# A 640-point spectral transform done as five residue tables instead of four quarter tables and a rest, on one Trainium2 core

## The chip, the cores and the metric

The kernel runs on one core of a Trainium2 chip. A core has five engines with their own instruction queues: TensorE (PE in the profile: matmuls into PSUM; its weight loads are listed apart as PEld), VectorE (DVE), ScalarE (ACT), GpSimd (POOL) and SyncE (SP), which here issues all transfers. Each engine works through its own queue strictly in the order in which the program was written, and an instruction whose input is not ready holds up everything behind it on that engine. The metric is device time in microseconds (us) from the start to the end of one launch. The kernel before takes 212.32 us (median of three runs, 211.74 to 212.51).

## The reference, cut to what matters

Inputs are bf16; x is 1 x 2048 x 640, the spectral weights are 2048 x 321, the feed-forward size is 1536.

```python
xn = layernorm(x)                                            # over the last axis, no gain
X  = rfft2(xn, axes=(-2, -1)) * (w_r + 1j * w_i)             # 2048 x 321, complex
s  = irfft2(X, s=(2048, 640)).astype(bf16)
g  = silu((gelu(xn @ w_gate) * (xn @ w_up)) @ w_down)        # 2048 x 640
return x + s * g
```

Two chains start from the normalised rows: a two-dimensional spectral filter and a gated feed-forward network (FFN). They meet in one product and one sum per element at the end.

## The kernel before

The 2048 rows are split into 16 slabs of 128 rows (row = 16 * n2 + n1; a slab holds one n1). The spectral chain per slab and per group is:

- `fold_a`, `fold_b` (L427, L435; VectorE, two slabs at a time): sums and differences of a row with its mirror images, which turn a 640-point transform along the columns into four real transforms of length 128 and a rest of 128 columns (`fold4`, L419).
- `slab_S1` (L470): five 128x128 matmuls, the transform along n2. ScalarE copies the result out of PSUM.
- `slab_D` (L489, matmuls in `d_matmuls` L479): the transform along the columns. For each of four output quarters one matmul with a 128x161 table `FT` and one with a table `TR` that adds the rest, so eight matmuls of 161 columns a slab. ScalarE copies the result (`zd`, L493), SyncE sends it to a scratch tensor `ZDR`.
- `quad_S2` (L507) and `quad_S2i` (L525), 16 times ("quads"): the 16-point transform over n1, the product with the weights (two VectorE products `p1`, `p2` a quad, L520), and the inverse 16-point transform. ScalarE copies both PSUM results (`xs` L516, `us` L536), and four transfers send `us` to the scratch tensor `UDR`.
- `vfold` (L553), `slab_S1i` (L568), `slab_Di` (L580): the way back, again with a fold, five 128x128 matmuls and eight 161-column matmuls a slab; then two VectorE operations spread the even and odd parts into the output tile `Y` (L587, L588).
- `finish` and `multiply_add` (L601, L594): when a slab of `Y` and of the gate G are both there, two VectorE operations (times G, plus x) and the output transfer follow at once.

The FFN is done in four groups of four slabs: 12 pairs of gate and up matmuls (`ffn_piece` L616: five matmuls of 512 columns each, Gelu on ScalarE into `ge` L628, the product `uT` on VectorE L630), then 4 x 3 `down_third` (L650: eight matmuls of 320 columns), with tanh on ScalarE and one product on VectorE for the gate (`gate_out`, L672; in the last group Silu on ScalarE, and there `multiply_add` comes directly after it).

The order of everything is written out by hand. The list `back` holds 144 steps of FFN work ("slots", numbered from 0); after each slot the items that `put(slot, ...)` has entered for it are emitted, in the order of the calls. So each queue is the slots in order with the spectral work dropped in between. Slots 0 to 35 are FFN group 0, 36 to 71 group 1, 72 to 107 group 2, 108 to 143 group 3. Before the change the forward spectral stage fills slots 3 to 58, the quads 66 to 91, the way back 100 to 134.

Buffers that matter: the PSUM pool `psB` has two buffers, used in turn by every PSUM result of the spectral chain; the FFN has two PSUM buffers for gate (`psg`) and two for up (`psu`), so the third `psu` in a row waits until VectorE has read the first.

```python
for s, b in enumerate(back):                 # L822
    b[0](*b[1:])
    if not any(it[0] is quad_S2 for it in plan[s]):
        flush()
    for it in plan[s]:
        it[0](*it[1:])
    flush()
```

Of the kernel before, what the change touches and what calls it, by code (L numbers as in the profile page):

```python
# [9 lines left out]
FP32 = mybir.dt.float32  # L10
# [65 lines left out]
def build(nc, env):  # L76
    consts, big, wts, xg, work, psA, psB = (env[k] for k in ("consts", "big", "wts", "xg", "work", "psA", "psB"))
# [53 lines left out]
    FT = consts.tile([P, 5, LH], BF16)  # L131
    TR = consts.tile([P, 2, 2, LH], BF16)
# [36 lines left out]
    lint = gtile([LH], INT32)  # L169
    nc.gpsimd.iota(lint, pattern=[[1, LH]], base=0, channel_multiplier=0)  # L170
    vt = gtile([NS, P], INT32)

# [21 lines left out]
    u_f, hi_f, s_f, h_f, g_f, pf, lo_b = bits("pb", [(0, 63), (6, 1), (0, 31), (5, 1), (5, 3), (0, 127), (0, 1)])  # L194
    ph_t = affine("ph_t", hi_f, -1536.0, 1536.0)
    e96 = c1("e96")
    nc.vector.tensor_single_scalar(out=e96, in_=pf, scalar=96.0, op=ALU.is_equal)
    a_m = affine("a_m", pf, 2.0, 64.0)
    b_o = affine("b_o", pf, 1.0, 32.0)
    sp_f = c1("sp_f")  # L200
    nc.vector.tensor_scalar(out=sp_f, in0=e96, scalar1=160.0, scalar2=s_f, op0=ALU.mult, op1=ALU.add)
    b_e = affine("b_e", h_f, -160.0, 160.0)
    a_r = affine("a_r", sp_f, 2.0, 0.0)
    b_r = c1("b_r")
    nc.vector.tensor_scalar(out=b_r, in0=sp_f, scalar1=hi_f, scalar2=b_e, op0=ALU.mult, op1=ALU.add)
# [39 lines left out]
    fv = gtile([3, LH], FP32)  # L245
    ftm = gtile([3, LH], FP32)

    def ft_angle():
        nc.scalar.activation(out=fv[:, 0], in_=lint, func=ACT.Identity, scale=a_m)
        nc.scalar.activation(out=fv[:, 1], in_=lint, func=ACT.Identity, scale=a_m, bias=b_o)  # L250
        nc.scalar.activation(out=fv[:, 2], in_=lint, func=ACT.Identity, scale=a_r, bias=b_r)
        nc.scalar.activation(out=ftm, in_=fv, func=ACT.Identity, scale=1.0 / 640.0, bias=magic)
        nc.scalar.activation(out=ftm, in_=ftm, func=ACT.Identity, bias=nmagic)

    def ft_wrap():
        nc.vector.scalar_tensor_tensor(out=fv, in0=ftm, scalar=-640.0, in1=fv, op0=ALU.mult, op1=ALU.add)

    def ft_sin():
        w = TWO_PI / 640.0 * (1.0 - 2e-7)
        nc.scalar.activation(out=ftm[:, 0:2], in_=fv[:, 0:2], func=ACT.Abs)  # L260
        nc.scalar.activation(out=FT[:, 1:4:2], in_=fv[:, 0:2], func=ACT.Sin, scale=w)
        nc.scalar.activation(out=FT[:, 4], in_=fv[:, 2], func=ACT.Sin, scale=w)
        nc.scalar.activation(out=FT[:, 0:4:2], in_=ftm[:, 0:2], func=ACT.Sin, scale=-w, bias=halfpi)

    def ft_rest():
        nc.gpsimd.memset(mhalf, -0.5)
        mk4 = consts.tile([P, 4], FP32)
        for g in range(4):
            nc.vector.tensor_single_scalar(out=mk4[:, g:g + 1], in_=g_f, scalar=float(g), op=ALU.is_equal)
        for g in range(4):  # L270
            nc.vector.tensor_scalar(out=TR[:, g // 2, g % 2, :], in0=FT[:, 4, :], scalar1=mk4[:, g:g + 1],
                                    scalar2=None, op0=ALU.mult)
        nc.gpsimd.memset(TR[32:33, 0, 0, 0:LH:2], 1.0)
        nc.gpsimd.memset(TR[32:33, 0, 0, 1:LH:2], -1.0)
# [144 lines left out]
    def fold4(dst, src, plus, minus):  # L419
        s4 = src.rearrange("p k (t d) -> p k t d", t=2)  # L420
        dm = dst[:, :, 0:512].rearrange("p k (g d) -> p k g d", g=4)
        dr = dst[:, :, 512:640].rearrange("p k (g d) -> p k g d", g=4)
        for gs, op in ((plus, ALU.add), (minus, ALU.subtract)):
            nc.vector.tensor_tensor(out=dm[:, :, gs, :], in0=s4[:, :, :, 32:160], in1=s4[:, :, :, 288:160:-1], op=op)
            nc.vector.tensor_tensor(out=dr[:, :, gs, 1:32], in0=s4[:, :, :, 1:32], in1=s4[:, :, :, 319:288:-1], op=op)

    def fold_a(pair):  # L427
        xn = X[:, 2 * pair:2 * pair + 2, :]
        assert ("n", 2 * pair + 1) in done
        uvt = work.tile([P, 2, D], BF16, tag="uv", bufs=1)  # L430
        nc.vector.tensor_tensor(out=uvt[:, :, 0:320], in0=xn[:, :, 0:320], in1=xn[:, :, 320:640], op=ALU.add)
        nc.vector.tensor_tensor(out=uvt[:, :, 320:640], in0=xn[:, :, 0:320], in1=xn[:, :, 320:640], op=ALU.subtract)
        xf[pair] = uvt

    def fold_b(pair):  # L435
        uvt = xf[pair]
        f = work.tile([P, 2, D], BF16, tag="xf", bufs=2)
        fold4(f, uvt, slice(0, 4, 3), slice(1, 3))
        nc.vector.tensor_copy(out=f[:, :, 512:D:32], in_=uvt[:, :, 0:D:160])
        xf[pair] = f  # L440
        done.add(("f", pair))

    def chunk(f, k, c):
        return f[:, k, c * P:(c + 1) * P]
# [25 lines left out]
    def slab_S1(n1):  # L470
# [3 lines left out]
        for c in range(5):  # L474
            nc.tensor.matmul(pz[:, c, :], lhsT=chunk(f, n1 % 2, c), rhs=Tfwd[:, n1, :], start=True, stop=True)  # L475
# [3 lines left out]
    def d_matmuls(ps, lhs):  # L479
        for b in range(2):  # L480
            for k in range(2):
                o = ps[:, b, k * LH:(k + 1) * LH]
                nc.tensor.matmul(o, lhsT=lhs[:, 2 * b + k, :], rhs=FT[:, 2 * b + k, :], start=True, stop=False)  # L483
                nc.tensor.matmul(o, lhsT=lhs[:, 4, :], rhs=TR[:, b, k, :], start=False, stop=True)  # L484

    def natural(ps):
        return ps[:, :, 0:LP].rearrange("p b (c m) -> p c m b", c=2)

    def slab_D(n1):  # L489
        pd = psB.tile([P, 2, 512], FP32, tag="b")  # L490
        d_matmuls(pd, Zt.pop(n1))
        zd = work.tile([P, 2, LP], BF16, tag="m2", bufs=3)
        nc.scalar.copy(out=zd.rearrange("p c (m b) -> p c m b", b=2), in_=natural(pd))  # L493
        nc.sync.dma_start(out=ZDR[:, n1].rearrange("c p l -> p c l"), in_=zd[:, :, 0:L])
# [12 lines left out]
    def quad_S2(j):  # L507
# [8 lines left out]
        nc.scalar.copy(out=xs, in_=px[:, :, 0:L])  # L516
        p1 = work.tile([P, 2, L], BF16, tag="p1", bufs=3)
# [7 lines left out]
    def quad_S2i(j):  # L525
# [9 lines left out]
        us = work.tile([P, 2, L], BF16, tag="m2", bufs=3)  # L535
        nc.scalar.copy(out=us, in_=pu[:, :, 0:L])  # L536
        for lo in range(2):
            to = uv[lo][:, j // 8, :, j % 8, :]
            nc.sync.dma_start(out=to[:, :, 0:L], in_=us[lo * 64:lo * 64 + 32, :, :])
            nc.sync.dma_start(out=to[:, :, L:D], in_=us[lo * 64 + 32:lo * 64 + 64, :, 1:320])  # L540
# [12 lines left out]
    def vfold(pair):  # L553
        V = st_c["V"][:, 2 * pair:2 * pair + 2, :]
        f = work.tile([P, 2, D], BF16, tag="xf", bufs=2)
        fold4(f, V, slice(0, 4, 3), slice(2, 0, -1))
# [162 lines left out]
    for n1 in range(4, NS):  # L719
        if n1 == 7:  # L720
            s += 2
# [138 lines left out]
```

## Time and profile before

| | us |
|---|---|
| median of three runs | 212.32 |
| the profiled execution's own time | 212.3 |
| span of the profiled execution (first to last instruction) | 210.5 |
| TensorE busy | 200.3 (95%) |
| VectorE busy | 138.2 (66%) |
| ScalarE busy | 127.7 (61%) |
| GpSimd busy | 19.2 (9%) |

The page of the profile gives busy time by engine, then the span in 40 slices (a digit is the busy share in tenths), the transfer queues, the chain of work that ended last, and the costliest groups of instructions. A group line reads: line of the kernel, engine, operation, output<-input, shape, count, then busy time, the mean duration of one in ns, and the idle time of the engine before it with what ended it. Matmuls and VectorE operations overlap their neighbours at the ends, so the distance from one start to the next is shorter than the duration when nothing is waited for. A timeline line reads: start, duration, engine, line, operation, and in brackets the idle time before it.

### The profile page before, as it was taken

The numbers are of one execution on the slowest core, as the hardware profiler recorded it, in microseconds if no ns is written. First come the engines' busy times: TensorE is split into PE (matmuls) and PEld (weight loads), VectorE is DVE, ScalarE is ACT, GpSimd is POOL, SyncE is SP. The second block draws the span as 40 slices with busy tenths as digits, with TensorE's granted clock in tenths as the row PEclk, the third lists the DMA queues.
The fourth block names the chain that finished last, engine by engine and source line by source line (L and its number), as shares of the span: only waits on it lengthen the run. The fifth ranks groups of instructions, "written<-read, shape, count | busy, mean of one in ns | idle before, by whom it ended". The sixth has DMA issues, their size and how long they took to land.

```text
span 210.5 us, 4486 instructions
## 1 busy us (share of the span) xinstructions
PE 200.3 (95%) x1600; PEld 125.5 (60%) x1600; DVE 138.2 (66%) x436; ACT 127.7 (61%) x215; POOL 19.2 (9%) x53
## 2 busy tenths in 40 slices
PE   0699999999999999999999999999999999999993
PEld 0389984567765555666644434347776556666773
DVE  8878977975975662252566755423769888994443
ACT  7656567599575666532677767732466665665721
POOL 8000128720004000000000000000000000000000
PEclk9999999999999999999999999999999999999999
DMA  5999955765946575739963232328913443332221
GB/s 159 337 361 366 361 159 137 159 165 147 175 78 164 134 175 124 195 120 205 221 131 82 64 86 67 88 68 247 340 42 96 121 120 101 97 93 65 63 78 47
DMA packets 37222, 31.79 MB, mean 151 GB/s; under 512 B 11344, under 2 KB 35024, under 8 KB 37072
## 3 DMA queue, kind: packets, MB, share of 16 engines
q1 hardware_dynamic: 37200, 31.51, 55.5%
q8 instruction: 12, 0.20, 0.4%
q14 instruction: 10, 0.08, 0.1%
HBM read 20.34 MB, written 7.87 MB: 134 GB/s over the span
## 4 chain that ended last, share of the span: by engine, by line
PE 95%; DVE 3%; ACT 1%; issue 0%; POOL 0%; POOLq 0%
PE psg L623 25%; PE psu L623 25%; PE psg L647 13%; PE psu L647 12%; PE pu L533 2%; PE pz L475 2%; PE py L484 2%; PE pd L484 2%; PE pd L483 2%; PE py L483 2%; PE pv L572 2%; PE px L513 2%; PE pw L279 1%; DVE st L371 1%; ACT Tinv L219 1%; PE pt L453 1%
## 5 line engine op out<-in xcount | busy, mean ns | idle before, releaser
L623 PE MATMUL psg<-xnT,Wg 128*128 128x512 bf16 (+1 forms) x275 | 61.5, 355 | 0.0
L623 PE MATMUL psu<-xnT,Wu 128*128 128x512 bf16 (+1 forms) x275 | 61.2, 354 | 0.0
L630 DVE TENSOR_TENSOR uT<-psu,ge 128x512 bf16<-128x512 f32 (+1 forms) x55 | 34.0, 618 | 26.3 <-PE psu L623 25.0
L647 PEld LDWEIGHTS <-uT 128*128 128x128 bf16 x396 | 37.2, 98 | 14.3 <-issue 0.5
L628 ACT ACTIVATE ge<-psg 128x512 bf16<-128x512 f32 (+1 forms) x55 | 30.0, 546 | 20.4 <-PE psg L623 18.9
L623 PEld LDWEIGHTS <-Wg 128*128 128x128 bf16 x275 | 25.6, 99 | 20.0 <-issue 2.3
L623 PEld LDWEIGHTS <-Wu 128*128 128x128 bf16 x275 | 25.6, 99 | 19.7 <-issue 1.8
L647 PE MATMUL psg<-Wd,uT 128*128 128x320 bf16 (+1 forms) x204 | 31.1, 295 | 0.0
L647 PE MATMUL psu<-Wd,uT 128*128 128x320 bf16 (+1 forms) x192 | 28.9, 295 | 0.0
L520 DVE TENSOR_TENSOR p<-xs,W 128x642 bf16<-128x642 bf16 x32 | 14.5, 493 | 9.7 <-ACT xs L516 9.4
L584 ACT ACTIVATE eo<-py 128x644 bf16<-128x644 f32 x16 | 11.3, 707 | 9.8 <-PE py L484 9.6
L516 ACT CAST xs<-px 128x642 bf16<-128x642 f32 x16 | 11.1, 694 | 9.2 <-PE px L513 5.8
L493 ACT CAST zd<-pd 128x644 bf16<-128x644 f32 x16 | 11.1, 694 | 6.0 <-PE pd L484 6.0
L371 DVE BATCH_NORM_STATS2 st<-X 128x6 f32<-128x320 bf16 x32 | 13.9, 477 | 0.0
L596 DVE TENSOR_TENSOR Yall<-Yall,G 128x640 bf16<-128x640 bf16 (+2 forms) x21 | 8.7, 412 | 7.7 <-ACT G L683 7.3
L477 ACT CAST Z<-pz 128x640 bf16<-128x640 f32 x16 | 11.0, 688 | 4.0 <-PE pz L475 4.0
L574 ACT CAST vs<-pv 128x640 bf16<-128x640 f32 x16 | 11.0, 688 | 2.0 <-PE pv L572 2.0
L536 ACT CAST us<-pu 128x642 bf16<-128x642 f32 x16 | 11.2, 700 | 0.9 <-PE pu L533 0.9
L678 DVE SCALAR_TENSOR_TENSOR G<-th,psg 128x320 bf16<-128x320 f32 x12 | 5.8, 482 | 8.8 <-ACT th L677 8.7
L677 ACT ACTIVATE th<-psu 128x320 f32<-128x320 f32 x12 | 5.3, 439 | 8.6 <-PE psu L647 8.5
L483 PE MATMUL py<-FT,vs 128*128 128x161 bf16 x64 | 10.5, 233 | 0.0
L483 PE MATMUL pd<-FT,Z 128*128 128x161 bf16 x64 | 10.5, 233 | 0.0
(140 smaller groups left out, 235.8 us busy)
## 6 DMA issues: line engine op xcount, KB each, us to landing
ZDR<-zd SPq DMA_DIRECT2D x16, 160.5 KB, 3.0
B<-ZDR SPq DMA_DIRECT2D x8, 321.0 KB, 7.2
xt<-in_A_x_dram SPq DMA_DIRECT2D x16, 160.0 KB, 2.4
Wg<-in_B_w_gate_dram SPq DMA_DIRECT2D x4, 480.0 KB, 7.4
Wu<-in_B_w_up_dram SPq DMA_DIRECT2D x4, 480.0 KB, 8.4
X<-in_A_x_dram SPq DMA_DIRECT2D x3, 640.0 KB, 9.1
Wd<-in_B_w_down_dram SPq DMA_DIRECT2D x1, 1920.0 KB, 13.9
Vin<-UDR SPq DMA_DIRECT2D x3, 640.0 KB, 7.6
```

The costliest lines, as they stand in the source:

```text
L371: nc.vector.bn_stats(out=st[:, k, :], in_=xr[:, k, :])
L477: nc.scalar.copy(out=Zt[n1], in_=pz)
L483: nc.tensor.matmul(o, lhsT=lhs[:, 2 * b + k, :], rhs=FT[:, 2 * b + k, :], start=True, stop=False)
L493: nc.scalar.copy(out=zd.rearrange("p c (m b) -> p c m b", b=2), in_=natural(pd))
L516: nc.scalar.copy(out=xs, in_=px[:, :, 0:L])
L520: nc.vector.tensor_tensor(out=pp, in0=xs, in1=WT[j // 8][:, :, j % 8, :], op=ALU.mult)
L536: nc.scalar.copy(out=us, in_=pu[:, :, 0:L])
L584: nc.scalar.activation(out=eo.rearrange("p c (m b) -> p c m b", b=2), in_=natural(py), func=ACT.Copy, scale=(2.0 if n1 >= 12 else 1.0) / ( ...
L623: nc.tensor.matmul(ps, lhsT=WT[:, c, t * P:(t + 1) * P], rhs=xnT[g][:, c, c0:c1_], start=(c == 0), stop=(c == 4))
L628: late.append(lambda: nc.scalar.activation(out=ge, in_=ps, func=ACT.Gelu_apprx_tanh))
L630: nc.vector.tensor_tensor(out=uT[g][:, t, c0:c1_], in0=ps, in1=cur["ge"], op=ALU.mult)
L647: nc.tensor.matmul(ph, lhsT=uT[g][:, t, j * P:(j + 1) * P], rhs=Wd[:, t, c0:c1_], start=(t == 0), stop=(t == NT - 1))
```

## The change

The transform along the columns is taken at half-sample points and split by residues modulo 5. A row of 640 becomes, by sums and differences with its mirror image, an even and an odd half of 320; each half is five blocks of 64. Sums and differences of the blocks and two combinations with the golden ratio (`TAU`, `NU`) leave five full chunks of 128 columns, and each chunk needs one matmul with one full 128x128 table. So `slab_D` and `slab_Di` have five matmuls of 128 columns instead of eight of 161. What goes with it:

- the forward fold has three steps, `fold_a`, `fold_b`, `fold_c`: 2 TENSOR_TENSORs of 640 elements; 2 TENSOR_TENSORs of 512 and 2 SCALAR_TENSOR_TENSORs of 512 (times a constant, plus a tensor, all bf16 in SBUF); 1 TENSOR_TENSOR of 512 and 2 of 256, each needing the one before;
- on the way back there is no `vfold` (the chunks come out of `UDR` as they are needed); after the tables, `spread_a` has 2 SCALAR_TENSOR_TENSORs and 2 TENSOR_TENSORs of 512, `spread_b` has 2 TENSOR_TENSORs of 512 and 2 of 640, a pair of slabs at a time, through a tile `E` with two buffers;
- `quad_S2i` brings `us` into the order of the residues while copying it out of PSUM: two ScalarE copies of 256 elements and a VectorE copy of 256 instead of one ScalarE copy of 642. The products `p1`, `p2` move behind it into a new item `quad_P`. The tiles for `zd` and `us` are three fixed buffers `ZB`;
- a new item `fi_turn` builds the inverse tables from the forward ones by five transposes on TensorE and three ScalarE copies. The rest table `TR` and its VectorE set-up go;
- `multiply_add` of slabs 0 to 11 is no longer done as soon as possible but at slots 106, 112, 118, 124, 130, 132 to 136, 138 and 139. The x tiles for it are kept in the space of `W1`, eight at a time;
- the slots move: folds and tables in new places (forward stage slots 3 to 56, quads 64 to 89, way back 97 to 131), the second Sin table of the forward stage (`tinv_sin`) from slot 22 to 21.

```diff
-    FT = consts.tile([P, 5, LH], BF16)
-    TR = consts.tile([P, 2, 2, LH], BF16)
+    FT = consts.tile([P, 10, 64], BF16)
+    FI = consts.tile([P, 5, P], BF16)
...
     def fold_b(pair):
-        uvt = xf[pair]
-        f = work.tile([P, 2, D], BF16, tag="xf", bufs=2)
-        fold4(f, uvt, slice(0, 4, 3), slice(1, 3))
...
+        W = xf[pair].rearrange("p a k (m d) -> p (a k) m d", d=64)
+        NM = work.tile([P, 2, 4, 2, 64], BF16, tag="nm", bufs=1, name="NM")
+        nm = NM.rearrange("p i q x d -> p q i x d")
+        for x, i0, i1 in ((0, slice(4, 2, -1), slice(1, 3)), (1, slice(0, 2), slice(3, 1, -1))):
+            nc.vector.tensor_tensor(out=nm[:, :, :, x, :], in0=W[:, :, i0, :], in1=W[:, :, i1, :], op=ALU.subtract)
+        f = work.tile([P, 5, 2, P], BF16, tag="xf", bufs=2, name="f")
+        fc = f[:, 1:5].rearrange("p (a c) k d -> p c a (k d)", c=2)
+        for c, g in ((0, TAU), (1, -NU)):
+            nc.vector.scalar_tensor_tensor(out=fc[:, c], in0=NM[:, 1].rearrange("p (a k) x d -> p a (k x d)", a=2), scalar=g,
+                                           in1=NM[:, 0].rearrange("p (a k) x d -> p a (k x d)", a=2),
+                                           op0=ALU.mult, op1=ALU.add)
...
-    def d_matmuls(ps, lhs):
-        for b in range(2):
-            for k in range(2):
-                o = ps[:, b, k * LH:(k + 1) * LH]
-                nc.tensor.matmul(o, lhsT=lhs[:, 2 * b + k, :], rhs=FT[:, 2 * b + k, :], start=True, stop=False)
-                nc.tensor.matmul(o, lhsT=lhs[:, 4, :], rhs=TR[:, b, k, :], start=False, stop=True)
...
     def slab_D(n1):
+        for c in range(5):
+            nc.tensor.matmul(pair_of(cols, *FWD[c]), lhsT=Z[:, c, :], rhs=block2(FTf, c), start=True, stop=True)
...
     def quad_S2i(j):
-        us = work.tile([P, 2, L], BF16, tag="m2", bufs=3)
-        nc.scalar.copy(out=us, in_=pu[:, :, 0:L])
+        us = ZB[j % 3].rearrange("p (h r q) -> p h r q", h=2, r=6)
+        nc.scalar.copy(out=us[:, :, 1:4:2, :], in_=residues(pu, 1, 1))
+        nc.scalar.copy(out=us[:, :, 2:5:2, :], in_=residues(pu, 4, -1))
+        nc.vector.tensor_copy(out=us[:, :, 0:6:5, :], in_=residues(pu, 0, 5))
...
+    def spread_a(pair):
+        E = st_c["E"]
+        Eb = E.rearrange("p k (a m d) -> p (k a) m d", a=2, d=64)
+        NM = work.tile([P, 2, 4, 2, 64], BF16, tag="nm", bufs=1, name="NM")
...
+        nc.vector.scalar_tensor_tensor(out=NM[:, 0].rearrange("p q x d -> p q (x d)"), in0=H, scalar=TAU, in1=G,
+                                       op0=ALU.mult, op1=ALU.add)
...
+    fold_at = ((3, 5, 7), (8, 10, 12), (19, 20, 22), (26, 28, 30), (32, 33, 35), (38, 41, 43), (45, 46, 48), (49, 50, 52))
+    s1_at = ((9, 10, 11, 12), (14, 15, 16, 17), (23, 24, 26, 27), (31, 32, 34, 35), (36, 38, 39, 41), (44, 45, 47, 48),
+             (49, 50, 51, 52), (53, 54, 55, 56))
...
     for j in range(NS):
         put(sb, quad_S2, j)
         if j > 1:
             put(sb, quad_S2i, j - 2)
+        put(sb, quad_P, j)
...
+    for p in range(8):
+        sd = vs0 + 4 * p + 5 if p < 7 else s
+        put(sd + 1, spread_a, p)
+        put(sd + 2, spread_b, p)
+    for n1, sl in enumerate((106, 112, 118, 124, 130, 132, 133, 134, 135, 136, 138, 139)):
+        put(sl, multiply_add, n1, 0, D)
+        if n1 < 8:
+            put(sl, load_xt, n1 + 8)
```

In the lists of the diff, `fold_at` gives the slots of the three fold steps of a pair of slabs, `s1_at` those of its two `slab_S1` and two `slab_D`.

## The prediction

> **What bounds the kernel now.** I read the page's busy times and slices first, then the chain of waits, then busy times by stretch, then the timeline for what one operation costs from its start to the next start.
>
> ```profile
> PE 200.3 (95%) x1600; PEld 125.5 (60%) x1600; DVE 138.2 (66%) x436; ACT 127.7 (61%) x215; POOL 19.2 (9%) x53
> DVE  8878977975975662252566755423769888994443
> PE 95%; DVE 3%; ACT 1%; issue 0%; POOL 0%; POOLq 0%
> ```
>
> TensorE is the bound: its slices are full from the third to the last but one, and the chain runs through it. VectorE is at two thirds, but unevenly: near 8 in the first third (the forward stage) and near 9 late (the way back), low between.
>
> ```profile
> 54.00:72.00 18.00, 18.00 (x128) 10.85 (x127) 12.88 (x36) 11.70 (x19) 2.33 (x6) 1.00 0.59 133
> 152.00:192.00 40.00, 40.00 (x316) 24.98 (x314) 33.49 (x106) 25.77 (x42) 0.00 (x0) 1.00 0.33 99
> ```
>
> The stretches say the same in us (length, then busy PE, PEld, DVE, ACT, POOL, granted clock): on the way back VectorE works 33.5 of 40. What is added to it has 6.5 us to go into, less what TensorE gives up.
>
> TensorE's prices, from the timeline: the first eight matmuls follow each other by 70 ns, the five chunks take 0.28 us.
>
> ```profile
> 59.78 0.23 PE L483 MATMUL pd<-FT,Z 128*128 128x161 bf16 x1
> 59.85 0.23 PE L484 MATMUL pd<-TR,Z 128*128 128x161 bf16 x1
> ...
> 60.34 1.24 PE L623 MATMUL psu<-xnT,Wu 128*128 128x512 bf16 x5
> 62.49 0.44 PE L475 MATMUL pz<-Tfwd,f 128*128 128x128 bf16 x5
> 62.77 1.24 PE L623 MATMUL psu<-xnT,Wu 128*128 128x512 bf16 x5
> ```
>
> VectorE's prices, a stretch without gaps, start to start: the FFN product 0.60, 640 elements 0.40, or 0.53 where the next needs the result; 512 elements are 0.35, or 0.46.
>
> ```profile
> 162.11 0.42 DVE L424 TENSOR_TENSOR f<-Vin 128x512 bf16<-128x512 bf16 x1
> 162.46 0.22 DVE L425 TENSOR_TENSOR f<-Vin 128x124 bf16<-128x124 bf16 x1
> ...
> 163.28 0.68 DVE L630 TENSOR_TENSOR uT<-psu,ge 128x512 bf16<-128x512 f32 x1
> 163.88 0.32 DVE L587 TENSOR_TENSOR Yall<-eo 128x321 bf16<-128x321 bf16 x1
> 164.11 0.32 DVE L588 TENSOR_TENSOR Yall<-eo 128x319 bf16<-128x319 bf16 x1
> 164.47 0.49 DVE L596 TENSOR_TENSOR Yall<-Yall,G 128x640 bf16<-128x640 bf16 x1
> 165.00 0.49 DVE L597 TENSOR_TENSOR Yall<-Yall,xt 128x640 bf16<-128x640 bf16 x1
> 165.41 0.68 DVE L630 TENSOR_TENSOR uT<-psu,ge 128x512 bf16<-128x512 f32 x1
> ```
>
> **The change part by part.** *TensorE.* Eight matmuls at 0.56 us become five at 0.28: 0.28 less in each of 32 slab steps, -9.0 us. `fi_turn` adds five transposes, +0.3. With every other engine hidden the span would be 210.5 - 9.0 + 0.3 = 201.8.
>
> *The new VectorE operation* is a SCALAR_TENSOR_TENSOR of 512 bf16 elements in SBUF, 32 in all. No row has it. The two nearest:
>
> ```profile
> L424 DVE TENSOR_TENSOR f<-uvt 128x512 bf16<-128x512 bf16 x16 | 6.8, 424 | 0.1
> L256 DVE SCALAR_TENSOR_TENSOR GEN<-GEN 128x483 f32<-128x483 f32 x1 | 0.7, 657 | 0.0
> ```
>
> At L256's pace, (657 - 155) / 483 = 1.04 ns an element over a fixed 155, it lasts 0.69 and costs 0.60 to the next start; at L424's, 0.42 and 0.35. I take 0.60, the row of the same operation, and keep 0.35 as the lower end. The Trainium skill ("Vector Engine (DVE) Microarchitecture Reference", 5.1 Performance modes) names copy, cast, tensor_scalar and tensor_tensor for the mode with two 16-bit elements a cycle and not this operation, a rule against this change; no row here can show it in bf16, and by the other reading the sum below would be 211.8.
>
> *VectorE's work.* A forward pair now costs 0.41 + 0.53 (`fold_a`), 0.35 + 0.46 + 2 x 0.60 (`fold_b`), 0.46 + 0.33 + 0.21 (`fold_c`) = 3.95 against 0.94 + 1.04 = 1.98 before: +15.8 over eight pairs, while the set-up of `TR` gives back 1.6, early. A pair on the way back costs 0.60 + 0.72 + 0.35 + 0.46 + 0.35 + 0.46 + 0.41 + 0.45 = 3.80, against 1.17 (`vfold`) + 2 x 0.60 = 2.37: +11.4. The 16 copies of `us` (256 f32 from PSUM) are bounded by the 128x256 product from PSUM at L630, 417 ns, and the 128x256 bf16 copy at L355, 284 ns; I take 0.42, the f32 row: +6.7.
>
> *Forward stage, slots 3 to 53.* The table matmul of a pair comes one or two slots after its `fold_c`, so VectorE can't fall behind by more than about a slot (1.08). I follow both queues from slot 6 of the timeline (20.1 us), with 1.05 a statistic (9.72 to 10.76), 0.34 a small product, 0.40 a gate product or norm. Slot 8: `uT` of slot 6 sits behind `fold_b` and ends at 23.3, and the third `psu` wants it at 22.8: 0.5 lost. The third pair in full: from 30.8, the end of the second `fold_c`, VectorE has 0.34, two products 1.2 by slot 17, four statistics 4.2, the wrap 0.6, two norms 0.8, two more products 1.2, fold 3.95, small 0.2, and 0.8 of waiting (for GpSimd's root and ScalarE's norm): 44.1. TensorE has ten slots and four table steps from 30.5, 10.8 + 1.1: 42.4. So 1.7 lost. The other pairs likewise: fourth 56.1 against 54.5 (two gate products wait for TensorE with the fold behind them, 2.2; the Sin table now loaded at slot 21 makes a Gelu reload come before slot 22's `ge`, 1.4 on ScalarE, mostly in that wait), fifth 63.6 against 62.65, sixth 74.9 against 73.35, seventh 82.1 against 81.4, last in time. Sum 0.5 + 1.7 + 1.6 + 0.95 + 1.55 + 0.7 = 7.0. Work alone, without any waits in VectorE's queue, is 51.3 against TensorE's 49.3 from slot 14 to 52, so the lower end is 2.0 + 0.5 = 2.5.
>
> *Quads.* Two fall in neighbouring slots, the next slot is free.
>
> ```profile
> 113.73 0.70 ACT L536 CAST us<-pu 128x642 bf16<-128x642 f32 x1
> 114.44 0.33 PE L513 MATMUL px<-B,MG 64*64 64x321 bf16 x4
> 114.60 0.45 PE L533 MATMUL pu<-p,N 64*64 64x321 bf16 x8
> ```
>
> The second `pu` needs the buffer that `us` empties at 114.43: 0.17 to spare. The two ScalarE copies (128x256 from PSUM, 387 ns at L628) end as late, at 114.40; VectorE's copy writes the same tile, waits for them, and ends at 114.9. TensorE waits 0.3 in seven such pairs: +2.1; without that order between the copies nothing, with a copy of 0.5 us 2.7. `p1`, `p2` come 0.9 later but are wanted three slots on, and the transfers start 0.45 later. Before, the first `Vin` is issued at 141.66 and lands in 3.1, 7.4 after the last `pu` (137.4); now that is 7.85, and `slab_S1i` of slot 97 comes 8.65 after it. The eight x loads stand behind `Vin` on SyncE and are wanted from slot 106. Those I cost at nothing; with 0.8 us more of transfer the cover is gone.
>
> *Way back and end, slot 103 on.* VectorE has eight pairs 30.4, twelve `multiply_add` at 0.94 11.3, the last group's seven halves and two quarters 5.3, twelve products 7.2, four gate products 1.6: 55.8, against TensorE's 41 slots and 27 table steps, 51.9. Followed in order, the last `uT` (slot 131) stands behind `spread_a` of pair 7 and a `multiply_add` and ends 3.3 after its matmul wants it, and the five `multiply_add` of slots 132 to 136 keep the last pieces late: the span ends 4.4 after TensorE alone would. Lower end, all spreads at 0.35 a new operation: 2.1. The twelve output transfers that come late (160 KB, 1.8 us to land) fill a quiet queue; nothing.
>
> *Start.* ScalarE's table work is shorter by 1.5, but Tinv (5.68) waits for VectorE; GpSimd's three small iotas for one take some 0.4 more, and its Tinv product (ends 3.9) has 1.1 to spare. Nothing.
>
> Sum: 201.8 + 7.0 + 2.1 + 4.4 = 215.3, and 1.8 outside the span (212.3 - 210.5) make 217.1, 2.3% above. The profiled 212.3 is the median, so nothing is shifted.
>
> **The rivals.** *The new operation at 0.35.* VectorE has 8.0 us less. Forward the losses become 0, 1.2, 1.3, 0.5, 0.9, 0.15 = 4.0, the end 2.1, quads as before: 201.8 + 8.2 + 1.8 = 211.8, within 0.5%, not slower. It decides from about 0.40 down. For it: every bf16 row of TENSOR_TENSOR. Against: L256, and the products from PSUM, all at 1.04 ns.
>
> *VectorE never waits in its own order.* Its queue runs ahead, forward costs 2.5, quads 0.5, end 3.8: 201.8 + 6.8 + 1.8 = 210.4, faster. For it: before, VectorE stood near 9 in the slices of the way back and no TensorE wait appears. Against: before, 25.0 us of its idle time at L630 is waiting for `psu`.
>
> *All is hidden:* 203.6. Against it 55.8 of work in 51.9.
>
> *TensorE slows after its waits.* The first matmuls of the kernel (L279, 6.88) take 0.46 each against 0.216 for 512 columns later: TensorE starts slow. A wait of 3.3 before the last group could bring that back over some 4.7 us (6.9 to 11.6), +2.4 at half pace: 219.5. For it the length of that wait; against, all others are under 2. The Trainium skill ("TensorE: Matmul & The Clock Gate", Part 1) puts the idle time that halves the clock at about 3.4 us; by it this one is just short; the trace of before has no such idle stretch once it has begun.
>
> **How the numbers follow.** As summed 0.62 (213.5 to 220.5), new operation at 0.35 0.16, no waits in order 0.09, all hidden 0.03, slow clock 0.10. The prediction is 217.1. The range, 210.4 to 220.0, takes in the first three cases but for the top of the first and the slow clock's. Half a per cent (1.1 us) is what a measurement can tell from no change. Faster: 0.09 + 0.03 + 0.04 of the rival at 0.35 = 0.16; same: 0.09 of that rival and 0.03 of the first case = 0.12; slower 0.72.
>
> **What would show it.** In the profile after: VectorE at 160 us or more; `f` and `NM` from SCALAR_TENSOR_TENSOR at about 687 ns; TensorE waiting for `f` before the table matmuls (six waits of 0.7 to 1.7), for the copy of `us` (0.3 each), for the last `uT` (3.3); slices of VectorE at 9 in both folding stages; the 128-column matmuls at 56 ns apart. A duration near 424 makes the forecast wrong by its largest term; waits of TensorE absent in the forward stage make the walk wrong.

## The result, and the profile after

The changed kernel takes 226.5 us (median of four executions, 224.92 to 228.69), against 212.23 for the kernel before in the same comparison: a ratio of 1.065, 95% interval 1.0587 to 1.0713. It is slower, as forecast, but by 14 us and not by 5. The profiled execution is the slowest of the four (228.69, span 226.8), and the ratio leaves it out, as it does every execution more than 1.5% above the fastest of its kernel, while the medians take in all of them. The account below is made against its span, which the forecast had at 215.3.

The page of the changed kernel: busy times, the slices of VectorE and of the granted clock, and the chain by engine.

```profile
PE 198.6 (88%) x1509; PEld 118.1 (52%) x1509; DVE 164.4 (72%) x429; ACT 126.3 (56%) x230; POOL 19.1 (8%) x58
DVE  6878893967798899261255767753139999999995
PEclk9999999969999999999599999999999999999999
PE 47%; DVE 26%; DMA 10%; issue 5%; SPq 4%; POOL 3%; ACT 3%; DVEq 0%; ACTq 0%
```

TensorE fell from 95% of the span to 88%, and the chain, which went through TensorE for 95%, now spends a quarter in VectorE, a tenth in transfers and some in the queues of SyncE and GpSimd. The row of the clock has two dips; that of the kernel before had none:

```profile
PEclk9999999999999999999999999999999999999999
```

Where TensorE waited (us in total, times, longest; the wait of 7 us before the first matmul, nearly as long before, is left out):

```profile
PE pz L504 <- DVE f L469: 8.3, 5, 4.4
PE px L539 <- DMA B<-ZDR: 3.3, 2, 2.3
PE psg L700 <- DVE uT L683: 2.8, 1, 2.8
PE pv L597 <- DMA Vin<-UDR: 1.3, 1, 1.3
PE psu L676 <- DVE uT L683: 0.5, 1, 0.5
```

The prices were as forecast. The group lines (count, then busy us and mean ns):

```profile
L458 DVE SCALAR_TENSOR_TENSOR f<-NM 128x512 bf16<-128x512 bf16 x16 | 10.4, 690 | 0.3
L568 DVE CAST zu<-pu 128x256 bf16<-128x256 f32 x16 | 6.8, 423 | 10.5 <-ACT zu L567 8.4
```

The new operation lasts 690 ns (forecast 687), the copy of `zu` 423 (forecast 0.42). So the trouble is in when things come. The same FFN matmuls start this much later than before:

| FFN matmul | before | after | later by |
|---|---|---|---|
| `psu` ahead of the third pair's tables | 42.10 | 40.44 | -1.7 |
| the next down-projection behind them | 44.54 | 49.17 | 4.6 |
| down-projection after the forward stage | 95.08 | 102.49 | 7.4 |
| the first back at full pace in the quads | 102.47 | 116.88 | 14.4 |
| after the last quads | 134.16 | 150.85 | 16.7 |
| way back begun | 148.16 | 166.46 | 18.3 |
| last `psu` | 190.97 | 205.62 | 14.7 |
| last of all | 206.25 | 221.93 | 15.7 |

Two steps carry it, 6.3 us around 45 us and 7.0 around 108 us. The way back gives back 3.6, as the cheaper tables should. The timeline of the changed kernel around the first step (start, duration, in brackets the idle time before):

```profile
32.05 0.19 POOL L317 TENSOR_SCALAR n1x<-mb 128x1 f32<-128x1 f32 x1 [21.83 <-DVE mb L194]
...
36.55 1.36 POOL L336 TENSOR_SCALAR vs<-kr,n1x,phs 128x16 int32<-128x16 int32 x4
38.27 1.04 POOL L420 TENSOR_TENSOR nrn<-ve,mhalf 128x4 f32<-128x4 f32 x1
39.34 0.45 DVE L432 TENSOR_SCALAR X<-X,mva,nrn 128x640 bf16<-128x640 bf16 x1 [3.58 <-POOL nrn L420]
46.08 0.63 PE L504 MATMUL pz<-Tfwd,f 128*128 128x128 bf16 x5 [4.40 <-DVE f L469]
46.50 2.34 PE L700 MATMUL psg<-Wd,uT 128*128 128x320 bf16 x8
```

The statistics of group 1 are done at 34.6, but GpSimd is in the eighteen small operations of `mg_phase` (slot 14) until 37.9 and comes to `root4(1)` (slot 16) only then. In the kernel before, `root4(1)` stood at slot 12, ahead of `mg_phase`, and its last operation ended at 31.9; the root itself is this line of that timeline:

```profile
30.26 1.04 POOL L403 TENSOR_TENSOR nrn<-ve,mhalf 128x4 f32<-128x4 f32 x1
```

VectorE waits 3.58 us for the root with the whole third pair behind it, TensorE then 4.40 for the pair, and the eight matmuls that follow take 2.14 us to the next start where 1.09 is usual. The second step:

```profile
95.20 0.62 SPq L112 DMA_DIRECT2D W<-in_A_w_i_dram  x1
98.40 0.56 SPq L124 DMA_DIRECT2D W<-W  x1
99.06 1.32 SPq L519 DMA_DIRECT2D ZDR<-zu  x2
102.78 5.18 SPq L530 DMA_DIRECT2D B<-ZDR  x8
107.12 0.33 PE L539 MATMUL px<-B,MG 64*64 64x321 bf16 x2 [2.29 <-DMA B<-ZDR]
108.47 0.47 PE L539 MATMUL px<-B,MG 64*64 64x321 bf16 x2 [1.03 <-DMA B<-ZDR]
108.88 2.32 PE L700 MATMUL psu<-Wd,uT 128*128 128x320 bf16 x8
```

On SyncE the copy W<-W waits 2.5 us for the load ahead of it, and the stores of the last two slabs stand behind it; they land, B's loads are issued, and TensorE stands. In the kernel before the first `px` followed on the matmul ahead of it without a wait:

```profile
99.52 0.48 PE L513 MATMUL px<-B,MG 64*64 64x321 bf16 x4
```

The busy times by stretch (length, then busy PE, PEld, DVE, ACT, POOL, and the granted clock) say what came after both waits:

```profile
46.40:49.80 3.40, 3.40 (x19) 2.26 (x18) 2.65 (x7) 1.53 (x3) 0.00 (x0) 0.53 0.24 48
108.00:114.60 6.60, 6.13 (x26) 3.05 (x26) 1.46 (x4) 1.83 (x3) 0.00 (x0) 0.51 1.07 224
...
163.00:203.00 40.00, 40.00 (x321) 25.02 (x320) 34.28 (x73) 27.13 (x46) 0.00 (x0) 1.00 0.30 98
```

Half the clock for 3.4 and for 6.6 us, worth some 1.7 and 3.0. The last line is the way back, where VectorE works 34.3 of 40 us and TensorE never waits until the last `uT`. The account of the span over TensorE alone (201.8):

| | forecast | measured |
|---|---|---|
| forward stage, third pair (`pz` 4.4 and `psu` 0.5; forecast 1.7) | 1.7 | 4.9 |
| forward stage, the rest | 5.3 | 3.9 |
| half clock after waits | 0 | 4.7 |
| first `px`, waiting for B | no term | 3.3 |
| quads | 2.1 | 2.3 |
| first `pv`, waiting for Vin | 0 | 1.3 |
| last `uT` 2.8, and the end 0.6 later behind TensorE's last matmul | 4.4 | 3.4 |
| sum | 13.5 | 23.8 |

201.8 + 23.8 = 225.6; the remaining 1.2 is in pieces that I have not assigned.

### The profile page after: what moved, and what is told of

Read it like the earlier page. It is cut to its first block, busy times and chain, and to the rows that moved or that the text cites. A ratio compares the mean times of both kernels' runs of the same rounds, so it can differ in the third digit from the quotient of the medians.

```text
span 226.8 us, 4340 instructions
## 1 busy us (share of the span) xinstructions
PE 198.6 (88%) x1509; PEld 118.1 (52%) x1509; DVE 164.4 (72%) x429; ACT 126.3 (56%) x230; POOL 19.1 (8%) x58
## 4 chain that ended last, share of the span: by engine, by line
PE 47%; DVE 26%; DMA 10%; issue 5%; SPq 4%; POOL 3%; ACT 3%; DVEq 0%; ACTq 0%
PE psu L676 13%; PE psg L676 12%; PE psu L700 6%; PE psg L700 5%; DVE uT L683 3%; SPq L573 3%; DVE Yall L653 3%; DVE f L458 3%; DMA W<-in_A_w_i_dram 2%; DMA B<-ZDR 2%; DVE st L388 2%; DMA UDR<-zu 2%; PE pv L597 2%; DVE NM L454 2%; PE pu L563 2%
## 5 line engine op out<-in xcount | busy, mean ns | idle before, releaser
L700 PEld LDWEIGHTS <-uT 128*128 128x128 bf16 x396 | 38.3, 102 | 19.0 <-DVE uT L683 3.1
L700 PE MATMUL psg<-Wd,uT 128*128 128x320 bf16 (+1 forms) x204 | 33.8, 313 | 2.8 <-DVE uT L683 2.8
L700 PE MATMUL psu<-Wd,uT 128*128 128x320 bf16 (+1 forms) x192 | 30.8, 302 | 0.0
L550 DVE TENSOR_TENSOR p<-xs,W 128x642 bf16<-128x642 bf16 x32 | 14.3, 489 | 6.9 <-DMA B<-ZDR 4.5
L504 PE MATMUL pz<-Tfwd,f 128*128 128x128 bf16 x80 | 7.6, 229 | 8.3 <-DVE f L469 8.3
L568 DVE CAST zu<-pu 128x256 bf16<-128x256 f32 x16 | 6.8, 423 | 10.5 <-ACT zu L567 8.4
L516 ACT CAST zu<-pd 128x640 bf16<-128x640 f32 x16 | 11.1, 691 | 4.8 <-PE pd L514 3.9
L731 DVE SCALAR_TENSOR_TENSOR G<-th,psu 128x320 bf16<-128x320 f32 x12 | 5.8, 484 | 9.3 <-ACT th L730 9.2
L504 PEld LDWEIGHTS <-f 128*128 128x128 bf16 x80 | 5.8, 102 | 12.6 <-DVE f L469 10.6
L615 ACT ACTIVATE E<-py 128x640 bf16<-128x640 f32 x16 | 11.2, 699 | 1.7 <-PE py L612 1.7
L458 DVE SCALAR_TENSOR_TENSOR f<-NM 128x512 bf16<-128x512 bf16 x16 | 10.4, 690 | 0.3
```

What stands on the lines that cost most here:

```text
L458: nc.vector.scalar_tensor_tensor(out=fc[:, c], in0=NM[:, 1].rearrange("p (a k) x d -> p a (k x d)", a=2), scalar=g, in1=NM[:, 0].rearrange ...
L504: nc.tensor.matmul(pz[:, c, :], lhsT=f[:, c, n1 % 2, :], rhs=Tfwd[:, n1, :], start=True, stop=True)
L516: nc.scalar.copy(out=zd[:, 1:2 * LP - 1].rearrange("p (c l) -> p c l", c=2)[:, :, 0:320] .rearrange("p c (q r) -> p c q r", r=5), in_=flat ...
L550: nc.vector.tensor_tensor(out=pp, in0=xs, in1=WT[j // 8][:, :, j % 8, :], op=ALU.mult)
L615: nc.scalar.activation(out=st_c["E"][:, n1 % 2, :], in_=flat, func=ACT.Copy, scale=(2.0 if n1 >= 12 else 1.0) / (S * D))
L700: nc.tensor.matmul(ph, lhsT=uT[g][:, t, j * P:(j + 1) * P], rhs=Wd[:, t, c0:c1_], start=(t == 0), stop=(t == NT - 1))
```

## The experiments

Theory A: the forecast's prices and its walk are right, and what was missed are two late arrivals, each by a queue in which something else stands ahead, and the half clock after them. Its rivals: VectorE's work alone makes everything late; or the slow matmuls have another cause than TensorE's waits. Spans carry along when the first loads come: the up matmuls of slot 2 start between 13.5 and 14.7 us. Where less than 1 us matters I compare the time from those matmuls to the end of the span, called the run below: 196.3 for the kernel before, 212.6 for the changed one.

**mg_phase out of the root's way.**

```diff
-    put(14, mg_phase)
+    put(9, mg_phase)
```

> mg_phase (18 small GpSimd operations, 5.9 us) enters at slot 9 instead of 14, so that root4(1) no longer stands behind it. Theory A (GpSimd's queue is what made the third pair's fold late): the root ends near 36.2 instead of 39.3, VectorE's wait of 3.58 at the norm goes to about 0.5, TensorE's wait of 4.4 for f falls to 1.3 to 1.8, the 0.48 at psu goes, and with no idle stretch over 2 us there the granted clock stays at 1.00 between 40 and 52 us: 3.1 + 1.7 = about 4.8 less, 226.5 to 221.7. Rival B (VectorE's longer fold alone makes the pair late, the root is hidden): the wait stays above 3.5 and the time within 1 us of 226.5. The wait for B at 105 us stays under both.

221.74 us (218.22 to 222.74), ratio 1.0352 (1.0274 to 1.0429). The profiled execution is the one of 218.22; its waits of TensorE, and the third pair:

```profile
PE pz L504 <- DVE f L469: 5.5, 5, 1.6
PE px L539 <- DMA B<-ZDR: 1.9, 2, 1.0
```

```profile
42.39 0.45 PE L504 MATMUL pz<-Tfwd,f 128*128 128x128 bf16 x5 [1.61 <-DVE f L469]
42.68 1.25 PE L700 MATMUL psg<-Wd,uT 128*128 128x320 bf16 x8
```

1.61, where the forecast had 1.7, and the matmuls behind it run at full pace. The median fell by 4.8 as theory A has it. The profiled execution has no dip of the clock at all, and its run is 202.4, 10.2 less: on SyncE the longest wait of a copy W<-W is 0.6 instead of 2.5, the wait for B fell to 1.9, and no dip followed it. Why the copy waits less is not shown. The other three executions are 2.6 to 4.5 us longer, with a granted clock of 0.985 to 0.992; where they lost it is not on record.

**Weight loads over fewer slots.**

```diff
-        put(d_slot[k * 14 // 40], *item)
+        put(d_slot[k * 12 // 40], *item)
```

> The 40 weight-load items are spread over the first 12 slab_D slots instead of 14, so that none stands on SyncE ahead of the stores of slabs 14 and 15. Theory A (the last store and so the load of B waited in SyncE's queue behind the weight copies): the last ZDR store is issued near 96.7 instead of 99.7, B's loads near 100.4 instead of 102.8, TensorE's waits at px fall from 3.3 to about 1.1, and the half clock at 108 to 114.7 goes: 2.2 + 3.4 = 5.6 less, about 220.9. Rival B (the eight loads of B are slow because of what else moves on the DMA engines, not because of their issue): the loads are issued earlier but land less than 1 us earlier; time within 1 us of 226.5. Rival C: the weight loads, now denser, make the X transposes on SyncE late and a new wait for them appears at a psg of the next group.

226.97 us (224.39 to 228.02): nothing gained. The profile shows the same third pair as the changed kernel's (a wait of 4.40 and the half clock behind it), so that step is not peculiar to the one execution above. B's loads are issued at 101.11, 1.0 earlier counted from the up matmuls of slot 2, but there is another wait in the way. The timeline of SyncE and ScalarE:

```profile
92.27 6.47 SPq L519 DMA_DIRECT2D ZDR<-zu  x4
97.44 0.69 ACT L516 CAST zu<-pd 128x640 bf16<-128x640 f32 x1 [2.66 <-DMA ZDR<-zu]
```

SyncE is still 3.9 us behind, so the store that empties the first of the three `ZB` buffers goes out only at 92.27 and takes 5.1 to land; ScalarE waits for it before it can write slab 15. TensorE waits 1.6 and 1.1 at `px`, and the half clock follows all the same; a third stretch of it follows the 2.78 at the last `uT`. Theory A named the right queue and the wrong cure.

**Both edits**, the two diffs above together.

> Both edits together. Theory A: the two gains add, 226.5 - 4.8 - 5.6 = 216.1, which is within 1 us of the time that was forecast (217.1), and the granted clock is 1.00 from 20 us to the end. If the gains hide behind one another (what one wait gives back the next takes), 219 to 221.

221.68 us (220.99 to 222.34), ratio 1.0452: no better than the first edit alone, since the second did not do what it should. Waits: 5.5 for f, 2.7 at `px`, and one dip of the clock after the latter.

**The waits left, TensorE kept busy in them.**

```diff
+    put(23, warm_up, 18)
     for sl, it in f_units.items():
...
+    put(sb, warm_up, 10)
     for j in range(NS):
         put(sb, quad_S2, j)
```

> Nothing of the waits is changed; 18 matmuls of 512 columns whose result is used by nobody stand ahead of the third pair's first table matmul and 10 ahead of the first px, 3.9 and 2.2 us of work where TensorE waited 4.4 and 2.3. Theory A (the half clock after these waits comes from TensorE's standing idle): the waits end when they ended before, but the matmuls behind them run at full pace (eight of 320 columns in 1.1 instead of 2.1 us) and the granted clock is 1.00: 1.7 + 3.4 = 5.1 less, 221.4. Rival B (the slow matmuls come from something else that happens at these times, the burst of transfers for example): the granted clock falls to 0.5 all the same, and the time stays within 1 us of 226.5.

222.27 us (222.03 to 222.56), 4.2 less than the changed kernel by unused work alone. The timeline of TensorE:

```profile
40.91 4.05 PE L296 MATMUL pw<-Tinv,ident 128*128 128x512 bf16 x18
45.47 0.45 PE L504 MATMUL pz<-Tfwd,f 128*128 128x128 bf16 x5 [0.51 <-DVE f L469]
45.76 1.25 PE L700 MATMUL psg<-Wd,uT 128*128 128x320 bf16 x8
...
204.05 0.31 PE L700 MATMUL psg<-Wd,uT 128*128 128x320 bf16 x1 [2.83 <-DVE uT L683]
204.20 2.25 PE L700 MATMUL psu<-Wd,uT 128*128 128x320 bf16 x12
206.25 3.05 PE L700 MATMUL psg<-Wd,uT 128*128 128x320 bf16 x12
```

The pair still comes late (45.47), but the matmuls behind it are fast, and the granted clock is 1.00 in both stretches. That TensorE's own standing idle brings the half clock is shown. The last two lines are the rest of it: this execution fell to half pace behind the 2.83 at the last `uT`, which the changed kernel's profile, with 2.82 at the same place, did not.

**The golden ratio left out.** From here on the kernels have `mg_phase` at slot 9, and 4 unused matmuls ahead of the first `px` and 10 behind slot 131 that hold the clock.

```diff
-            nc.vector.scalar_tensor_tensor(out=fc[:, c], in0=NM[:, 1].rearrange("p (a k) x d -> p a (k x d)", a=2), scalar=g,
...
-                                           op0=ALU.mult, op1=ALU.add)
+            nc.vector.tensor_tensor(out=fc[:, c], in0=NM[:, 1].rearrange("p (a k) x d -> p a (k x d)", a=2),
+                                    in1=NM[:, 0].rearrange("p (a k) x d -> p a (k x d)", a=2), op=ALU.add)
```

and the two in `spread_a` likewise.

> The kernel with mg_phase at slot 9 (span 216.4 where the clock stayed at 1.00), with 4 unused matmuls ahead of the first px and 10 behind slot 131 so that the clock stays up, and with the 32 SCALAR_TENSOR_TENSORs replaced by TENSOR_TENSORs of the same tiles: the multiplication by the golden ratio is left out. Theory A (VectorE's work is what the remaining waits come from, and the new operation at 0.60 start to start costs 0.25 more than a TENSOR_TENSOR): VectorE's busy time falls by 32 x 0.27 = 8.5 us to about 156; the five waits for f fall from 5.5 to 3.0 or less, the last group's wait from 2.8 to about 1; span 216.4 - 4.3 = about 212. Rival B (the waits come from VectorE's place in the order, behind GpSimd, ScalarE and TensorE, not from its work): waits for f stay above 4.5 and the span above 215.

217.06 us (216.02 to 220.79). VectorE's busy time is 156.9, and TensorE's waits:

```profile
PE pz L503 <- DVE f L468: 2.5, 3, 1.1
PE pz L503 <- ACT ge L678: 0.7, 1, 0.7
```

The waits for f fall from 5.5 to 3.2 and the last `uT` comes 1.1 after TensorE wants it in place of 2.8 (1.1 of the 2.2 us of unused matmuls there is then pure cost). The run is 200.3 against 202.4, without that cost 3.2 less; I expected 4.3. So the new operation's 0.25 a piece is a good part of the loss. It is not all: even at TENSOR_TENSOR's price the kernel stays behind the one before, and of what is left a part is VectorE's other added work (the 3.2 at `pz`) and a part waits for transfers. The rival that put the kernel at 211.8 at that price was too low as well: 200.3 - 1.1 + 14.2 + 1.8 = 215.2, of which 3.3 are the waits for B and Vin that it did not have.

**The copies W<-W behind the next block's loads.**

```diff
-                todo += [(w_plus, i, b, half, ri) for ri in range(2)] + [(w_dup, i, b, half)]
+                todo += [(w_plus, i, b, half, ri) for ri in range(2)] + held
+                held[:] = [(w_dup, i, b, half)]
...
-    for k, item in enumerate(filt(0) + filt(1)):
-        put(d_slot[k * 14 // 40], *item)
+    for k, item in enumerate(filt(0) + filt(1) + held):
+        put(d_slot[k * 12 // 40], *item)
```

> mg_phase at slot 9 and the same unused matmuls, and the eight W<-W copies on SyncE each entered behind the next block's loads, all 40 items over the first 12 slab_D slots. Theory A (SyncE waits at the copies for loads just issued, and the ZDR stores stand behind them): SyncE's waits at the copies (L124, 4.8 us in all in the changed kernel) go to under 1, the last two ZDR stores are issued when zu is there, B's loads near 95.3 instead of 96.2, TensorE's waits at px 1.9 less 0.9: span about 215.5. Rival B (SyncE is behind because its issues of 0.6 each fill the time, whatever their order): B's loads at 96 or later, and the span within 0.5 of 216.4.

217.09 us (216.57 to 217.98), ratio 1.0259 (1.0204 to 1.0313); the clock stays at 1.00. SyncE and TensorE:

```profile
94.53 5.16 SPq L530 DMA_DIRECT2D B<-ZDR  x8
99.11 1.03 PE L296 MATMUL pw<-Tinv,ident 128*128 128x512 bf16 x4
100.07 0.44 PE L539 MATMUL px<-B,MG 64*64 64x321 bf16 x4
```

B's loads are issued 1.3 earlier than with the first edit alone, counted from the up matmuls of slot 2, and behind 0.9 us of unused matmuls there is no wait left. Against the kernel with both first edits, which has the same twelve slots and the copies in their old place, they are issued 2.0 earlier, counted likewise. The profiled executions of this kernel and of the one with the first edit alone, both without a dip, differ by 1.3 (201.1 against 202.4); the rest of the 4.7 between the medians is in executions that have no profile. With both queues mended and the clock held by unused matmuls the changed kernel takes what was forecast for it. That the figure is met is luck: misses of both signs cancel.

**The multiply_adds on GpSimd.**

```diff
-        nc.vector.tensor_tensor(out=Y, in0=Y, in1=Gt[n1 // 4][:, n1 % 4, c0:c1_], op=ALU.mult)
+        (nc.vector if n1 >= 12 else nc.gpsimd).tensor_tensor(out=Y, in0=Y, in1=Gt[n1 // 4][:, n1 % 4, c0:c1_], op=ALU.mult)
```

and the addition of x likewise.

> mg_phase at slot 9, the same unused matmuls, and the multiply_adds of slabs 0 to 11 on GpSimd instead of VectorE. Theory A (at the end VectorE's work is the bound): VectorE loses 24 operations, 11.3 us; the wait of 2.8 for the last uT goes and the last pieces come sooner: span about 213 (216.4 - 2.8 - 0.6, and 10 unused matmuls, 2.2 us, then cost what of them no longer lies in a wait, so up to 215). Rival B (GpSimd takes over 2.5 us an operation, or VectorE's operations grow longer beside it): the output of slabs 8 to 11 comes after TensorE's end, span above 217.

238.06 us, ratio 1.1245: the slowest of all, as rival B has it. The groups:

```profile
L653 POOL TENSOR_TENSOR Yall<-Yall,G 128x640 bf16<-128x640 bf16 x12 | 19.4, 1618 | 79.1 <-DVE Yall L644 79.1
L626 DVE SCALAR_TENSOR_TENSOR NM<-E 128x512 bf16<-128x512 bf16 x8 | 12.6, 1580 | 0.0
L630 DVE TENSOR_TENSOR E<-E,NM 128x512 bf16<-128x512 bf16 x8 | 9.9, 1233 | 0.3
L683 DVE TENSOR_TENSOR uT<-psu,ge 128x512 bf16<-128x512 f32 (+1 forms) x55 | 33.5, 618 | 15.1 <-PE psu L676 13.1 <-ACT ge L681 2.0
```

GpSimd needs 1.6 us for what VectorE does in 0.49, and VectorE's operations beside it stretch, in the mean of their groups, from 0.69 to 1.58 and from 0.42 to 1.23. VectorE's busy time rose by 12, although 24 operations had gone, and TensorE waits 14.3 us for `uT`.

**fold_a on GpSimd.**

```diff
-            nc.vector.tensor_tensor(out=T[:, par].rearrange("p k (m d) -> p k m d", d=64), in0=up, in1=down, op=op)
+            nc.gpsimd.tensor_tensor(out=T[:, par].rearrange("p k (m d) -> p k m d", d=64), in0=up, in1=down, op=op)
```

> mg_phase at slot 9, the same unused matmuls, and the two TENSOR_TENSORs of 640 of fold_a on GpSimd. GpSimd's nearest row is a TENSOR_SCALAR of 1024 int32 in 1.2 us, so some 0.8 each. Theory A: VectorE loses 7.5 us in the forward stage, the waits for f fall from 5.5 to about 2, span about 213. Rival B: GpSimd takes two or three times VectorE's time, fold_b waits for it, the waits for f grow; span 217 to 222.

221.3 us (219.37 to 222.42). An operation takes 1.4 us, as its group says:

```profile
L446 POOL TENSOR_TENSOR T<-X 128x640 bf16<-128x640 bf16 x16 | 22.0, 1395 | 32.4 <-DVE f L469 23.5 <-ACT X L428 5.4 <-DVE X L432 3.6
```

The waits for f grow from 5.5 to 8.2: `fold_b` waits 7.7 us for GpSimd. Rival B.

**All norms of groups 1 to 3 on ScalarE.** On top of the kernel of 217.09.

```diff
-            put(nf[p], norm, 2 * pair)
+            put(nf[p], norm_act, 2 * pair)
```

> The kernel with mg_phase at slot 9, the W<-W copies late and the unused matmuls (span 214.7, waits for f 5.6), and the six norms of groups 1 to 3 that VectorE does (L432, 0.44 each) on ScalarE, which then does all twelve. Theory A (VectorE's work in the forward stage sets the waits for f): VectorE has 6 x 0.36 = 2.2 us less, the waits for f fall from 5.6 to 3.5 to 4, span about 213. Rival B (a pair's fold waits for its norms, and two norms one behind the other on ScalarE at 0.92 come later than one on each engine): VectorE waits at fold_a for ScalarE, the waits for f stay within 0.7 of 5.6 or grow, span 214 to 217.

218.01 us (217.16 to 218.93). The waits at `pz` sum to 5.3 where they were 5.6: VectorE's 2.2 us less work bought 0.3. That is rival B's outcome; its mechanism, the fold waiting for a norm on ScalarE, shows in the third pair alone (0.64 us), and what holds the other pairs is not shown. And the third pair's wait, now the longest,

```profile
43.34 0.64 PE L504 MATMUL pz<-Tfwd,f 128*128 128x128 bf16 x5 [1.99 <-DVE f L469]
43.78 2.34 PE L700 MATMUL psg<-Wd,uT 128*128 128x320 bf16 x8
```

brought the half clock after only 1.99 us of idling.

**The quads' third copy, left out and moved.** Again on top of the kernel of 217.09.

```diff
-        nc.vector.tensor_copy(out=us[:, :, 0:6:5, :], in_=residues(pu, 0, 5))
```

> The same kernel of span 214.7 without VectorE's copy of residues 0 and 5 in quad_S2i (L568; those columns of zu stay zero). In it TensorE falls back by 0.3 in each pair of neighbouring quads, 2.0 us over the quads. Theory A (the second pu of a pair waits for the copy, which comes after both of ScalarE's): the 0.3 steps go, TensorE's lateness against the kernel before grows by under 0.3 over the quads, span 214.7 - 2.0 = 212.7. Rival B (the buffer comes free late because of ScalarE's two copies alone): 0.1 or more of each 0.3 stays, span 213.5 or above.

```diff
-        nc.vector.tensor_copy(out=us[:, :, 0:6:5, :], in_=residues(pu, 0, 5))
+        nc.scalar.copy(out=us[:, :, 0:6:5, :], in_=residues(pu, 0, 5))
```

> The same kernel of span 214.7 with the copy of residues 0 and 5 on ScalarE behind its other two. Theory A (what costs is the chain of three copies in a row, with a hand-over to VectorE): ScalarE starts it 0.1 sooner, the steps of 0.3 become 0.2, span about 214.0. Rival B (ScalarE, with 0.26 to 0.39 more in each quad, brings xs and ge later): steps of 0.4 or more, span 215.5 or above.

214.91 us without the copy, 216.06 (215.65 to 216.47; ratio 1.0185, 1.015 to 1.0219) with it on ScalarE; the runs are 198.9 and 200.1 against 201.1. The second of two neighbouring quads, with VectorE's copy:

```profile
113.56 0.33 PE L539 MATMUL px<-B,MG 64*64 64x321 bf16 x4
114.02 0.47 PE L563 MATMUL pu<-p,N 64*64 64x321 bf16 x8
```

and without it:

```profile
114.07 0.33 PE L539 MATMUL px<-B,MG 64*64 64x321 bf16 x4
114.23 0.45 PE L563 MATMUL pu<-p,N 64*64 64x321 bf16 x8
```

From `px` to `pu` 0.46 with the copy on VectorE, 0.16 without it, and 0.28 with it on ScalarE. So each pair loses 0.30 by that copy, as forecast, and 0.18 of it is VectorE's taking over from ScalarE rather than the copying. Without the copy theory A holds (span 213.0, expected 212.7); on ScalarE a step of 0.12 is left, less than either theory had.

**The put-off multiply_add behind the last uT.** On the kernel of 216.06.

```diff
-    for n1, sl in enumerate((106, 112, 118, 124, 130, 132, 133, 134, 135, 136, 138, 139)):
+    for n1, sl in enumerate((106, 112, 118, 124, 131, 132, 133, 134, 135, 136, 138, 139)):
```

> The kernel with all three mends (mg_phase at slot 9, W<-W copies late, third copy of zu on ScalarE; span 214.7) with the multiply_add of slab 4 at slot 131 instead of 130, so that it no longer stands on VectorE ahead of the last uT, and 6 unused matmuls behind slot 131 instead of 10. Theory A (from slot 103 on VectorE's work as a whole is the bound, and the wait of 2.8 for the last uT is only where it shows): uT ends 1.0 sooner, TensorE's wait there (what the unused matmuls cover and what is left) falls from 2.8 to 1.8 and TensorE ends up to 1.0 sooner, but VectorE works without a gap to its last operation and the span ends within 0.3 of where it did relative to the last psu. Rival B (the put-off multiply_add in front of uT is what the end costs): the span is 1.0 shorter, 213.7.

217.11 us (216.93 to 217.73). The last `uT` is in fact 0.9 sooner (1.3 us of unused matmuls and 0.56 of waiting, against 2.2 and 0.6), and TensorE is done 0.9 sooner after its last `psu`, yet the span ends 1.9 later relative to it. VectorE's timeline has the reason:

```profile
202.36 0.33 DVE L654 TENSOR_TENSOR Yall<-Yall,W 128x320 bf16<-128x320 bf16 x1 [1.85 <-DMA W<-in_A_x_dram]
```

The x tile of slab 12 lies where that of slab 4 was and is loaded only after slab 4's `multiply_add`; VectorE waited 1.85 for it, the only gap of more than 0.1 us in its work there, and the end came 1.9 later. The expectation had missed that wait. The point itself is as theory A has it: at the end a gap in VectorE's work costs its full length, and 0.9 us gained on TensorE gains nothing. That the end would have stayed where it was without the gap is worked out (1.9 less 1.85), not run.

No kernel here beats the one before; the best that leaves nothing out is 1.85% behind it.

## Why the prediction was right or wrong

Right: TensorE's saving (0.28 a slab step, and 0.28 for `fi_turn`), the 690 ns of the new operation, the quads' 0.30 a pair, and, with the root on time, the third pair's 1.7 (1.61). VectorE as the main reason why the new kernel is slower holds when the two queues are mended and the clock is held: it then takes 217.09, with 5.6 us of waits for f, the copy's 0.30 a pair and the late last `uT`; leaving out the golden ratio took 3.2 off the run of the kernel with the first edit, the unused matmuls' cost apart. The Trainium skill's rule that was weighed ("Vector Engine (DVE) Microarchitecture Reference", 5.1) held: the SCALAR_TENSOR_TENSOR in bf16 got no faster mode, 690 against 424 ns of a TENSOR_TENSOR of that size.

Wrong, in the order of their size:

- *The clock.* The rival "TensorE slows after its waits" got 0.10 and was set aside with "all others are under 2". They were not: 4.40 and 2.29 + 1.03. 4.7 us, shown by keeping TensorE busy in the waits (4.2 less). The wait that the rival had in mind, for the last `uT`, was 2.82 and brought no half clock in this execution.
- *The end of the forward stage: no term at all.* The prediction went from the forward stage to the quads' own steps and never followed the last store, the eight loads of B and the first `px`. `slab_D(14)` and `slab_D(15)` came two slots sooner than before and the quads with them, and SyncE's queue ahead of the last stores had not become shorter. 3.3 us; 1.4 of it went with the first edit, and with the copies W<-W out of the stores' way at most 0.9 is left, under the unused matmuls.
- *"0.8 of waiting (for GpSimd's root and ScalarE's norm)"* in the third pair. It was 3.58 for the root. The prediction looked at which slot `root4` was moved to and not at what it was moved past on GpSimd: `mg_phase`, 5.9 us long. 3.2 us; gone with one changed slot number.
- *Vin at nothing, "with 0.8 us more of transfer the cover is gone".* The first `pv` waited 1.3. The forecast had the transfers start 0.45 later, by the longer copy. But the first load of Vin is issued 7.2 after the last `pu` where it was 4.3 before: the last store of `us` leaves SyncE's queue 4.6 after the last copy, before 2.1. What filled that queue is not shown, and the other experiments have between 0 and 1.4 of this wait.
- *Terms too high:* the third `psu` of slot 8 did not wait (0.5 forecast), the fourth and sixth pairs' tables waited 1.28 and 1.07 and not 1.6 and 1.55, and the end cost 3.4 and not 4.4. These waits are the same when the third pair is on time (1.29 and 1.10).

The range failed because the losses were taken as a sum of small terms with their own errors; a wait over 2 us can bring the half clock with it, and that case was forecast for one wait alone, at 219.5, with 0.10.

## What to carry to other kernels

When a step moves to another slot, list for every engine it issues on what it now stands behind, not only how late its own inputs are: 3.2 and 3.3 us here came from queues of engines that are 8% busy or do no arithmetic. A TensorE wait of 2 us or more can have half clock behind it, which cost 1.7 to 3 us here, and unused matmuls in such a wait are a cheap way to see how much of a loss that is. Where an engine works without a gap to the end, moving one of its pieces out of TensorE's way gained nothing here; what has to go is work on that engine.

## What the runs showed of the hardware

The half clock does not need 3.4 us of idling. It came after waits of 4.40, of 1.99, and of 1.61 and 1.06 with 0.3 us of matmuls between them; of five waits of 2.78 to 2.83 at the same place, for the last `uT` in five profiled kernels, two brought it and three did not; the forward stage's single waits of 1.61 or less never did in a profiled execution. The Trainium skill ("TensorE: Matmul & The Clock Gate", Part 1) has the clock halved after an idle window of about 3.4 us that runs freely, whatever the kernel does. The length of the first dip agrees (3.4 us), and so does that the same wait falls differently from one execution to the next; that a window must be idle as a whole does not.

GpSimd's TENSOR_TENSOR of 640 bf16 elements takes 1.4 to 1.8 us, and while it runs VectorE's operations with both inputs in SBUF take up to three times as long in the mean of a group (0.42 to 1.23), but not the product `uT`, which has one input in PSUM: two of them took 1.28 us in the midst of GpSimd's work, 0.60 a piece as ever. The Trainium skill ("SBUF — State Buffer", Who interferes with whom) says that a VectorE instruction with two SBUF inputs contends with a GpSimd instruction that reads SBUF, and one with at most one SBUF input, outside its two-port modes, does not; the trace agrees on both.
